# VectorE's blocks of a gated attention pair move into the score ring, local logits move one tile ahead, and the gate moves into the denominators

## The chip, the cores and the metric

The kernel runs on one core of one Trainium2 chip. The time is the device time of one execution in microseconds (us). Engines are written as in the profile: PE is TensorE (PEld its weight loads), ACT is ScalarE, DVE is VectorE, POOL is GpSimd, SP is the engine that issues the DMAs. Each engine works through a queue of its own in order, and they meet by semaphores.

## The reference

Two attention layers over the same 2048 rows of 512 numbers, with 32 heads of 16 each, are mixed by a gate per row. A is full attention, B looks at eight earlier rows, two apart. B's input is not `B_x` but the same `x`.

```python
x = A_x                                             # [1, 2048, 512], bf16
g = sigmoid((x * gate_w).sum(-1, keepdims=True))
# A: q, k, v = x @ A_wqkv, 32 heads of 16
a = softmax(q @ k.T * 16 ** -0.5) @ v               # per head, 2048 x 2048
a = a.reshape(B, S, D) @ A_wo
# B: q, k, v = x @ B_wqkv; row s sees rows s, s - 2, ..., s - 14 (those >= 0)
b = softmax(where(mask, q . k[s - 2 * w], -1e9) * ...) over w, times v[s - 2 * w]
b = b.reshape(B, S, D) @ B_wo
return g * a + (1 - g) * b
```

## The kernel before

**Layer A.** The rows are cut into 4 chunks of 512 queries, the heads into 8 groups of 4. A *period* is one chunk and one group, so there are 32 periods, chunk by chunk. In a period there are 64 *blocks*: one head's scores of 128 keys (16 key tiles) against 512 queries. A block's scores are one matmul with 32 rows of weights (`kt_all`) and fill one PSUM bank; four such matmuls on different rows of the array can run at once. Keys lie in partitions and queries along the free axis, so the exponentials need no transposition before they are multiplied with the values. A value tile has 16 columns and a column of ones, so that row 17 of the accumulator `acc` collects the denominators.

**The ring.** Scores for ScalarE go in turn into a set of three banks (`rA`) and a set of two (`rB`) (line 19, `qk` and `ex` at lines 962 to 971). ScalarE takes a set in one instruction (`pT<-ring`). The eight banks of PSUM are 3 + 2 for the ring, one for `acc`, and two under the name `misc`, through which everything else goes: projections of Q, K, V, of layer B, of the output, transposes, and the scores of VectorE's blocks.

**VectorE's blocks.** From period 4 on, 4, 8 or 12 of the 64 blocks (`n_dve`, 264 of 2048 in all, of the last three key tiles) get their exponential on VectorE (`d_group`, line 983). Each block's scores are a matmul into a `misc` bank (`dq`). `p1` turns them into a 16-bit logarithm in `dt` (128x512, one instruction a block). Four blocks make a group. Four shifts of it (`sh`, 128x2048, `pd<-dt`), each rounded to a bf16 pattern, are weighted by four copies of the values (`vd_all`) and added up in `acc`: 16 matmuls a group.

**End of a period.** VectorE transposes `acc` (`po1`), takes the reciprocal of the denominators and multiplies (`po2`), and transposes back once in two periods (`po3`). The output projection of layer A (`a_part`) is evicted with a factor `g` per row (`a_ev`, tile `fa`), that of layer B (`b_part`) is added (`b_ev`), and the sum is stored.

**Layer B** (`b_tile`, line 721) has 16 tiles of 128 rows. K and V are projected, evicted to `kvs` and stored in DRAM (`kv_scr`); the shifted rows are loaded from there (`ksh`, `vsh`, each in two halves of four shifts). GpSimd multiplies and adds up the logits (`logits_half`, tile `lg`, 128x256), VectorE takes maximum and difference (`sm_pre`, which starts with `mx`), ScalarE the exponential (`sm_exp`, in `lg`), VectorE sum, reciprocal and product (`sm_post`), GpSimd multiplies the values (`av_half`). The factor 1 - g is in `sm_post`. TensorE transposes the result for the output projection (`fin`, eviction `oe`).

**The gate.** One row of `x @ gate_w` per chunk is written to DRAM by way of VectorE (`zrow`), read back as 16 rows of 128, transposed, and goes through ScalarE's exponential (`zsig`) and three small VectorE instructions (`zgate`).

**The order.** Nothing is issued where it stands in the code. Each step becomes an `Op` with an engine, an estimated duration, a due time, and the buffers that it takes and frees. `list_schedule` (line 137) plays the estimates through: each time it takes the engine that can start first and on it the op with the earliest due time among those that can start soon. The result is a fixed order for each engine's queue; estimates have no other effect on the run. Where the planner sees TensorE idle or only little used, it adds matmuls on zeros (`idle`, `put`, `zeros`). Due times of layer A come from `UNIT` (us a block) and `T0`; those of layer B's tile t from `B0 + t * BSP`:

```python
CFG = dict(
    set_sizes=(3, 2),
    ...
    b_start=32.0,
    b_space=46.7,
```

All instructions of an engine are recorded in one helper line (292 for most, 301 for matmuls), so the profile is read by tile names.

Of the kernel before, what the change touches and what calls it, by code (L numbers as in the profile page):

```python
# [18 lines left out]
    set_sizes=(3, 2),  # L19
    n_dve=(0,) * 4 + (4, 8) * 2 + (8, 12) * 12,  # L20
    dve_tiles=3,
    b_start=32.0,
    b_space=46.7,
# [18 lines left out]
NPT = 3  # L42
# [39 lines left out]
WAVE = lambda n: PASS * n  # L82
AHEAD = dict(pe=0.10, dve=0.12, act=0.25, pool=0.5, sp=0.0)
# [53 lines left out]
def list_schedule(ops, zeros):  # L137
# [40 lines left out]
    out, extra = [], []  # L178
    while len(out) < len(ops):
# [37 lines left out]
        if e == "pe":  # L217
            o.t, end = arr.put(o, t)
            o.done = end + LAT[e] + o.lat
        else:  # L220
            occ = o.occ(t) if callable(o.occ) else o.occ
            o.t, o.done = t, t + max(occ, o.lat)
            free[e] = t + occ
        cand[e].remove(o)
        out.append(o)
        for s_ in succ.get(o, ()):
            left[s_] -= 1
            if left[s_] == 0:
                s_.ready = max([s_.rel] + [d.done for d in s_.deps] + [d.t for d in s_.after])
                cand[s_.eng].append(s_)  # L230
# [4 lines left out]
def kernel(  # L235
# [23 lines left out]
    SZ = cfg["set_sizes"]  # L259
# [6 lines left out]
    def misc_ps(shape, dtype=FP32, tag="misc"):  # L266
        return ps.tile(shape, dtype, tag=tag, bufs=2 if tag == "misc" else 1, name="misc_ps")
# [50 lines left out]
    def op(eng, occ, fn, dl, **kw):  # L318
        o = Op(eng, occ, fn, dl, **kw)
        ops.append(o)  # L320
        return o
# [8 lines left out]
    B0, BSP = cfg["b_start"], cfg["b_space"]  # L330
    UNIT = 0.445
# [4 lines left out]
    dorder = [(t, j) for t in range(NT - 1, NT - 1 - NTD, -1) for j in range(4)]  # L336
    n_dve = cfg["n_dve"]
    units, first_unit = [], []
    for pi, (c_, i) in enumerate(periods):
        dset = set(dorder[:n_dve[pi]])  # L340
        first_unit.append(len(units))
        units += [(pi, t, j) for t in range(NT) for j in range(4) if (t, j) not in dset]
    first_unit.append(len(units))
    sets = []
    u = 0
    while u < len(units):
        n = SZ[len(sets) % 2]
        sets.append(units[u:u + n])
        u += n
    S0 = [T0 + UNIT * f for f in first_unit]  # L350

    def in_b(t):
        return B0 <= t < B0 + 16.5 * BSP

# [9 lines left out]
    z_scr = tc.dram_tile([S], FP32, name="z_scr")  # L364
# [3 lines left out]
    identf = const.tile([NT, NT], FP32, name="identf")  # L368
# [12 lines left out]
    negk = const.tile([128, NG], FP32, name="negk")  # L381
    ott2 = const.tile([128, 2, BPC, 32], BF16, name="ott2")
    g_sp = const.tile([128, NT], FP32, name="g_sp")
    omg = const.tile([128, NT], FP32, name="omg")
# [54 lines left out]
    def load_w(part):  # L439
        def s():  # L440
            if part == 0:
                wst["q"] = work.tile([128, NGR, QW], BF16, name="wst", tag="pd", bufs=NPD)
                out = wst["q"][:]
            else:
                out = wkv[:, :, (part - 1) * D:part * D]
            SP.dma_start(out=out, in_=a_w3[:, :, part * D:(part + 1) * D])
        return s
# [6 lines left out]
    def load_wo():  # L454
        SP.dma_start(out=bwo[:], in_=B_wo.rearrange("(c p) n -> p c n", p=128))
        wo4 = A_wo.rearrange("(a e j d) n -> j e d a n", e=2, j=4, d=DH)
        for j in range(4):
            for e in range(2):
                SP.dma_start(out=woarr[32 * j + DH * e:32 * j + DH * (e + 1), :, :], in_=wo4[j, e])
        SP.dma_start(out=kv_scr[0:16, :], in_=zst["z"][0:16, :])  # L460
# [12 lines left out]
    o_wo = op("sp", 5.5, load_wo, -8.2, deps=[o_wz], use=[zt], lat=24.0)  # L473
# [25 lines left out]
    o_warm = op("pe", 4.0, warm, -9.0, deps=[o_init_d], alloc=[tok("misc", 2)])  # L499
# [34 lines left out]
    def k_proj(i, sc, tag, dl, rel=0.0):  # L534
        st = {}
        tk = tok(tag, 2 if tag == "misc" else 1)
# [16 lines left out]
    def k_bound(i, dl):  # L553
        st = {}
        tk = tok("misc", 2)
# [5 lines left out]
        def sw():  # L561
            st["p"] = misc_ps([128, 2])
# [21 lines left out]
    for i in range(NG):  # L584
        o_kc[i] = []
        for sc in range(NC):
            if i == 0:
                o_kc[i].append(k_proj(i, sc, ("misc", "acc", "misc", "misc")[sc], -2.0 + sc))
            else:
                o_kc[i].append(k_proj(i, sc, "misc", S0[i] - 8.0 - 4.5 * (NC - 1 - sc), rel=S0[i - 1] - 6.0 if i > 1 else 10.0))  # L590
        k_bound(i, 2.0 if i == 0 else S0[i] - 5.0)


    o_v = {}

    def v_proj(h0, h1, tb, TB, tag, dl, rel=0.0):
        n = (h1 - h0) * DH
        st = {}
        tk = tok(tag, 2 if tag == "misc" else 1)
# [12 lines left out]
        def ev():  # L612
            V.tensor_copy(out=vp_all[:, tb:tb + TB, h0:h1, 0:DH], in_=st["pv"][:].rearrange("p t (h d) -> p t h d", d=DH))
            for t in range(max(tb, NT - NTD), tb + TB):
                for m in range(NV):
                    V.tensor_scalar(out=vd_all[:, m, t - (NT - NTD), h0:h1, :], in0=vp_all[:, t, h0:h1, :],
                                    scalar1=WEIGHTS[m] * 2.0 ** -DEXP, scalar2=None, op0=ALU.mult)
        xs = [o for sc in range(NC) if sc * TPC < tb + TB and (sc + 1) * TPC > tb for o in o_xt[sc]]
        a = op("pe", 0.62, mk(0), dl - 2.0, full=2, deps=[o_wv] + xs, alloc=[tk], rel=rel, name=f"vp{h0}.{tb}")
        b = op("pe", 0.62, mk(1), dl - 1.4, full=2, deps=[a], use=[tk])  # L620
        c = op("dve", 0.61 + 0.9 * max(0, min(TB, tb + TB - (NT - NTD))), ev, dl, deps=[b, o_init_p], use=[tk])
        for h in range(h0, h1):
            for t in range(tb, tb + TB):
                o_v[(h, t)] = c

    v_proj(0, 4, 0, 8, "misc", 3.0)
    v_proj(0, 4, 8, 8, "misc", 4.0)
# [9 lines left out]
    def q_proj(pi, tag, dl, rel=0.0):  # L637
        c_, i = periods[pi]
        st = {}
        tk = tok(tag, 2 if tag == "misc" else 1)  # L640
# [29 lines left out]
    o_zd = []  # L670
    for sc in range(NC):
        st = {}
        tk, tz = tok("misc", 2), tok("accT", 2)

        def zc(sc=sc, st=st):
            st["p"] = misc_ps([1, QW])
            for c in range(DC):
                mm(st["p"][0:1, :], gw[:, c:c + 1], xT[:, c, sc * QW:(sc + 1) * QW], c == 0, c == DC - 1, tile_position=(0, 0))

        def ze(st=st):  # L680
            zr = work.tile([128, BPC, 32], FP32, name="zrow", tag="accT", bufs=2)
            st["z"] = zr[0:1].rearrange("p b d -> p (b d)")
            V.tensor_copy(out=st["z"], in_=st["p"][0:1, :])

        def zd(sc=sc, st=st):
            SP.dma_start(out=z_scr[sc * QW:(sc + 1) * QW].rearrange("(o n) -> o n", o=1), in_=st["z"])
        dl = 32.0 + 2 * sc
        a = op("pe", 0.9, zc, dl, full=4, deps=[o_bw] + o_xt[sc], alloc=[tk], rel=22.0)
        b = op("dve", 0.61, ze, dl + 1, deps=[a], alloc=[tz], use=[tk])
        o_zd.append(op("sp", 0.6, zd, dl + 2, deps=[b], use=[tz]))  # L690
    st_g = {}
    tzr, tzp = tok("zrows", 1), tok("misc", 2)

    def zfin():
        st_g["zrows"] = work.tile([NT, 128], FP32, name="zrows", tag="zrows", bufs=1)
        SP.dma_start(out=st_g["zrows"][:], in_=z_scr.rearrange("(t p) -> t p", p=128))

    def ztr():
        st_g["zp"] = misc_ps([128, NT])
        chain(nc.tensor.transpose(out=st_g["zp"][:, 0:NT], in_=st_g["zrows"][:], identity=identf[0:NT, 0:NT]))  # L700
# [8 lines left out]
    a = op("sp", 0.6, zfin, 41.0, deps=o_zd, alloc=[tzr], lat=3.0)  # L709
    a = op("pe", 0.15, ztr, 42.0, deps=[a, o_init_p], alloc=[tzp], use=[tzr])  # L710
    a = op("act", 0.25, zsig, 43.0, deps=[a], use=[tzp])
    o_g = op("dve", 0.8, zgate, 44.0, deps=[a])
# [8 lines left out]
    def b_tile(t):  # L721
        st = {}
        tb = B0 + t * BSP
# [24 lines left out]
        tk = tok("misc", 2)  # L748
        a = op("pe", WAVE(2), proj("pk", 1, 0), tb - 34, full=2, deps=[o_bw] + o_xt[cb], alloc=[tk, tkv], rel=rel)
        a = op("pe", WAVE(2), proj("pk", 1, 2), tb - 33.5, full=2, deps=[a], use=[tk])  # L750
        ka = op("dve", 0.61, ke, tb - 33, deps=[a], use=[tk, tkv])
        tk = tok("misc", 2)
        a = op("pe", WAVE(2), proj("pv", 2, 0), tb - 32, full=2, deps=[o_bw] + o_xt[cb], alloc=[tk], rel=rel)
        a = op("pe", WAVE(2), proj("pv", 2, 2), tb - 31.5, full=2, deps=[a], use=[tk])
        va = op("dve", 0.61, ve, tb - 31, deps=[a, ka], use=[tk, tkv])
        o_kvd.append(op("sp", 0.6, kvd, tb - 30, deps=[va], use=[tkv], lat=3.0))
# [5 lines left out]
        tk = tok("misc", 2)  # L762
        a = op("pe", WAVE(2), proj("pq", 0, 0), tb - 24, full=2, deps=[o_bw] + o_xt[cb], alloc=[tk, tqb], rel=rel)
        a = op("pe", WAVE(2), proj("pq", 0, 2), tb - 23.5, full=2, deps=[a], use=[tk])
        qa = op("dve", 0.61, qe, tb - 23, deps=[a], use=[tk, tqb])
# [10 lines left out]
        kvd_ = o_kvd[max(0, t - 1):t + 1] + [o_wo]  # L776
        lk = [op("sp", 0.7, load("ksh", 0, hf), tb + (-24, 4)[hf], deps=kvd_, alloc=[tks[hf]], lat=7.0) for hf in range(2)]
        lv = [op("sp", 0.7, load("vsh", 1, hf), tb + (18, 30)[hf], deps=kvd_, alloc=[tvs[hf]], lat=7.0) for hf in range(2)]

        def logits_half(hf):  # L780
            def s():
                if hf == 0:
                    st["lg"] = work.tile([128, H, W], FP32, name="lg", tag="lg", bufs=2)
                ksh, lg, qb = st["ksh", hf], st["lg"], st["qb"]
                prod = work.tile([128, WP, D], FP32, name="prod", tag="prod", bufs=1)
                pv_ = prod[:].rearrange("p w (h d) -> p w h d", d=DH)
                for wp in range(0, WH, WP):
                    for w_ in range(WP):
                        for c0 in range(0, D, HB):
# [418 lines left out]
```

## Time and profile before

| | |
|---|---|
| Time, median of 3 runs | 916.61 us (915.06 to 917.93) |
| The profiled execution | 922.33 us, span of the core 920.6 us |
| Granted clock of TensorE, mean | 0.942 |
| ScalarE busy | 824.5 us (90%), of it 815.5 in 714 exps of the ring |
| TensorE busy (modelled) | 787.3 us (86%) |
| GpSimd busy | 777.8 us (84%) |
| VectorE busy | 686.9 us (75%) |
| DMA | 47.34 MB, 51 GB/s over the span |

A group's row has its busy time, the mean duration of one instruction, and the idle time of its engine just before such instructions with what ended most of it. Instructions of one engine overlap at their ends, so a group's busy time is a little less than the count times the mean. TensorE's busy time is modelled. A row of the waits names who waited, for whom, how long in total, how often, and the longest. The granted clock is TensorE's share of full speed.

### The profile page before, as it was taken

What the parts mean: (1) busy time and instruction counts of PE and PEld (TensorE: products, weight loads), DVE (VectorE), ACT (ScalarE), POOL (GpSimd) and SP (SyncE); (2) the same over time, 40 slices, a digit from 0 to 9 for tenths busy, and PEclk for the clock granted to TensorE, in tenths of its full rate; (3) what the DMA queues carried; (4) which work ended last, traced back from release to release, by engine and by line L of the source; (5) the groups of instructions that cost most, each with busy time, mean ns of one, the idle gap of its engine ahead of it and who ended that gap; (6) DMA issues with size and microseconds to landing.
All of it is one profiled execution on the core that took longest, in us unless ns stands there. A gap on an engine that the chain in (4) does not pass through costs nothing. (4 is left out here: it accounts for less than half of the span.)

```text
span 920.6 us, 18113 instructions
## 1 busy us (share of the span) xinstructions
PE 787.3 (86%) x7025; PEld 249.3 (27%) x7025; DVE 686.9 (75%) x1107; ACT 824.5 (90%) x736; POOL 777.8 (84%) x1088
## 2 busy tenths in 40 slices
PE   8988989898888898887878888798888988888787
PEld 4333323233222222222222222222222222213122
DVE  4456484856867978898878878778877978888766
ACT  2999999996989999999988979889988979889796
POOL 4559998997989788799998979999799989999840
PEclk9999999998989999999998999989997989979799
DMA  8310202021020002102020110201210111200000
GB/s 272 109 59 24 82 24 81 23 69 36 24 81 12 30 23 88 58 23 81 25 80 29 31 63 29 80 24 37 68 59 23 59 58 35 81 20 28 1 1 24
DMA packets 44477, 47.34 MB, mean 51 GB/s; under 512 B 2372, under 2 KB 41812, under 8 KB 44392
## 3 DMA queue, kind: packets, MB, share of 16 engines
q1 hardware_dynamic: 44392, 46.19, 15.6%
q8 instruction: 55, 0.90, 0.4%
q14 instruction: 30, 0.25, 0.1%
HBM read 39.86 MB, written 6.33 MB: 50 GB/s over the span
## 5 line engine op out<-in xcount | busy, mean ns | idle before, releaser
L292 ACT ACTIVATE pT<-ring 128x1536 bf16<-128x1536 f32 x714 | 815.5, 1320 | 52.8 <-PE ring L301 33.7
L301 PE MATMUL ring<-qt,kt_all 32*128 32x512 bf16 x1784 | 295.6, 397 | 80.2 <-ACT pT L292 75.1
L292 POOL TENSOR_TENSOR prod<-prod 128x256 f32<-128x256 f32 x352 | 269.2, 772 | 10.0
L292 DVE TENSOR_SCALAR pd<-dt 128x2048 uint16<-128x2048 uint16 x264 | 258.1, 1020 | 5.2 <-PE acc L301 3.6
L301 PE MATMUL acc<-pT,vp_all 128*17 128x512 bf16 (+1 forms) x1784 | 233.4, 401 | 1.3 <-DVE accT L292 1.2
L292 POOL TENSOR_TENSOR prod<-vsh,lg 128x256 f32<-128x256 bf16 x256 | 185.7, 755 | 45.7 <-issue 35.2
L292 POOL TENSOR_TENSOR prod<-ksh,qb 128x256 f32<-128x256 bf16 x256 | 188.7, 767 | 33.2 <-DMA ksh<-kv_scr 20.7
L292 DVE TENSOR_SCALAR dt<-misc 128x512 uint16<-128x512 f32 x264 | 172.6, 684 | 52.1 <-PE misc L301 37.6
L301 PEld LDWEIGHTS <-kt_all 32*128 32x128 bf16 x2048 | 98.8, 91 | 368.8 <-issue 358.9
L301 PE MATMUL acc<-pd,vd_all 128*17 128x512 bf16 x1056 | 105.5, 394 | 13.0 <-DVE pd L292 12.8
L301 PE MATMUL misc<-qt,kt_all 32*128 32x512 bf16 x264 | 92.3, 402 | 10.6 <-DVE dt L292 6.5
L301 PE MATMUL acc<-z 128*32 128x512 bf16 x276 | 99.4, 423 | 0.0
L301 PEld LDWEIGHTS <-vp_all 128*17 128x17 bf16 (+1 forms) x1784 | 53.8, 89 | 70.0 <-issue 55.9
L301 PE MATMUL misc_ps<-bw,xT 128*128 128x512 bf16 x192 | 61.1, 412 | 8.2 <-DVE dt L292 7.9
L292 POOL TENSOR_TENSOR ob<-ob,prod 128x256 f32<-128x256 f32 x64 | 54.0, 845 | 5.0
L301 PEld LDWEIGHTS <-vd_all 128*17 128x17 bf16 x1056 | 27.8, 88 | 64.2 <-issue 60.3
L301 PE MATMUL misc_ps<-xT,wq 128*32 128x512 bf16 x512 | 41.3, 389 | 0.0
L301 PE MATMUL misc_ps<-xT,wkv 128*32 128x512 bf16 x384 | 39.6, 385 | 1.9 <-DVE vp_all L292 1.0
L301 PEld LDWEIGHTS <-z 128*32 128x32 bf16 x312 | 26.1, 99 | 53.9 <-issue 45.6
L301 PEld LDWEIGHTS <-xT 128*128 128x128 bf16 x512 | 28.8, 100 | 41.7 <-issue 38.0
L301 PE MATMUL misc_ps<-xT,wk 128*32 128x512 bf16 x128 | 36.9, 386 | 0.0
L292 DVE CAST kvs<-misc_ps 128x512 bf16<-128x512 f32 x32 | 22.0, 688 | 19.8 <-PE misc_ps L301 19.5
(78 smaller groups left out, 510.0 us busy)
## 6 DMA issues: line engine op xcount, KB each, us to landing
ksh<-kv_scr SPq DMA_DIRECT2D x32, 512.0 KB, 4.4
vsh<-kv_scr SPq DMA_DIRECT2D x32, 512.0 KB, 4.0
kv_scr<-kvs SPq DMA_DIRECT2D x16, 256.0 KB, 2.6
xld<-in_A_x_dram SPq DMA_DIRECT2D x4, 512.0 KB, 8.7
out_dram<-osb SPq DMA_DIRECT2D x16, 128.0 KB, 1.7
bw<-in_B_wqkv_dram SPq DMA_DIRECT2D x1, 1536.0 KB
wkv<-in_A_wqkv_dram SPq DMA_DIRECT2D x2, 512.0 KB, 9.0
wst<-in_A_wqkv_dram SPq DMA_DIRECT2D x1, 512.0 KB, 8.5
```

What stands on the lines that cost most here:

```text
L292: return chain_on(key, f(*a, **k))
L301: return chain(nc.tensor.matmul(out, lhsT=lhsT, rhs=rhs, start=start, stop=stop, **kw))
```

## The change

- **Ring.** Both ring sets have three banks; `misc` has one bank. In each of 264 sets the third bank holds one block of VectorE's, at most one a set, spread over the period (`SPREAD`). ScalarE takes the first two banks of such a set, VectorE's `p1` the third (`d_set`, which replaces `d_group`). `SPREAD` and the last three key tiles set which block goes where. The block's scores are one of the set's three matmuls; there is no matmul into `misc` for it.
- **Buffers.** `pT` has 5 buffers in one pool in place of 3 + 3. From period 8 on, the space of the projection weights `wkv`, which are used up by then, holds two more `dt`, so that there are three.
- **Layer B.** The logits of both halves are due before the tile's date, a whole tile ahead of the values (`L1`, `KL`), and the planner allows for margins around the softmax (`SM_LAT`). GpSimd's steps are planned in pieces; its instructions are the same. Loads wait for the zero rows of `kv_scr` alone and no longer for the output weights, whose load moves behind.
- **Gate.** It is computed in columns by 64 small matmuls, without DRAM. 16 more spread it to the layout of the denominators (`g_rw`); `po2` multiplies the reciprocals by it. The output projections of A and B then add up in one accumulation (`ab_part`) with one eviction.
- **Planner.** Other estimates (`BESIDE`, `UNDER`: VectorE's shifts and GpSimd slow each other), due times and spacing (`UNIT`, `b_space`). The built program has 683 exps of the ring (418 of three banks, 265 of two) for 714, and 671 matmuls on zeros for 312.

```diff
-    set_sizes=(3, 2),
+    set_size=3,
...
-    b_start=32.0,
-    b_space=46.7,
+    b_start=40.0,
+    b_space=(41.0,) * 4 + (44.5,) * 4 + (47.5,) * 8,
...
-NPT = 3
+NPT = 5
+LATE0 = 8
+NDL = 3
+SPREAD = (0.85, 0.95)
...
+L1, KL, SM_LAT = -13.0, (-24.0, -20.0), (1.0, 1.0, 0.3, 1.0)
+SH_LAT = 0.3
+BESIDE, UNDER = 0.575, 0.52
...
+P1D, SHD = -100.0, 1.0
...
-        return ps.tile(shape, dtype, tag=tag, bufs=2 if tag == "misc" else 1, name="misc_ps")
+        return ps.tile(shape, dtype, tag=tag, bufs=1, name="misc_ps")
...
-    UNIT = 0.445
+    UNIT = 0.465
...
+            if len(cur) == SZ - 1 and due < n and due < n * taken / (SPREAD[n // 12] * total):
...
+                    cur.append((pi, *dl_[due][1], gi))
...
+    dt_bufs = [dt_a[:]] + [b_.bitcast(U16) for b_ in spare[:NDL - 1]]
...
+    def zmm(sc):
+        def s():
+            if sc == 0:
+                st_g["zp"] = misc_ps([128, NT])
+            for t in range(sc * TPC, (sc + 1) * TPC):
+                for c in range(DC):
+                    mm(st_g["zp"][:, t:t + 1], xT[:, c, t * 128:(t + 1) * 128], gw[:, c:c + 1], c == 0, c == DC - 1)
...
-        kvd_ = o_kvd[max(0, t - 1):t + 1] + [o_wo]
-        lk = [op("sp", 0.7, load("ksh", 0, hf), tb + (-24, 4)[hf], deps=kvd_, alloc=[tks[hf]], lat=7.0) for hf in range(2)]
+        kvd_ = o_kvd[max(0, t - 1):t + 1] + [o_zr]
+        lk = [op("sp", 0.7, load("ksh", 0, hf), tb + KL[hf], deps=kvd_, alloc=[tks[hf]], lat=7.0) for hf in range(2)]
...
-        l0 = op("pool", 11.6, logits_half(0), tb - 14, deps=[lk[0], qa], alloc=[tlg], use=[tks[0], tqb], name=f"lg{t}")
-        l1 = op("pool", 11.6, logits_half(1), tb + 18, deps=[l0, lk[1]], use=[tks[1], tqb, tlg])
-        a = op("dve", 0.95, sm_pre, tb + 19, deps=[l1], use=[tlg])
-        a = op("act", 0.36, sm_exp, tb + 18, deps=[a], use=[tlg])
-        a = op("dve", 1.95, sm_post, tb + 21, deps=[a, o_g], use=[tlg])
-        a0 = op("pool", 10.1, av_half(0), tb + 40, deps=[a, lv[0]], alloc=[tob], use=[tlg, tvs[0]])
+        l0 = chain_ops(lgs[0], tb - 14, [lk[0], qa], [tlg], [tks[0], tqb])
+        l1 = chain_ops(lgs[1], tb + L1, [l0, lk[1]], [], [tks[1], tqb, tlg])
+        a = op("dve", 0.95, sm_pre, tb + SMD, deps=[l1], use=[tlg], lat=0.95 + SM_LAT[1])
+        l1.lat += SM_LAT[0]
+        a = op("act", 0.36, sm_exp, tb + SMD, deps=[a], use=[tlg], lat=0.36 + SM_LAT[2])
+        a = op("dve", 1.95, sm_post, tb + SMD, deps=[a, o_g], use=[tlg])
+        a0 = chain_ops(avs[0], tb + 40, [a, lv[0]], [tob], [tlg, tvs[0]])
...
+    def d_set(pi, gi, t, j, st, q_, tr_, tn):
...
+        def p1():
+            V.tensor_scalar(out=g["dt"][:, n_, :], in0=st["r"][:, q_, :], scalar1=float(DH) ** -0.5 * RES / LN2,
+                            scalar2=(127.0 + DEXP + SHIFT * float(DH) ** -0.5 / LN2) * RES, op0=ALU.mult, op1=ALU.add)
...
+        o = op("dve", 0.61, p1, tn + P1D, deps=deps, alloc=[g["td"]] if first else [], use=[tr_] + ([] if first else [g["td"]]),
+               after=[d_last[0]], name=f"p1_{pi}")
...
+        def dur(t):
+            return 0.605
...
-        tp = tok("pT" + ring, NPT)
+        tp = tok("pT", NPT)
...
+            V.tensor_tensor(out=rden[:], in0=rden[:], in1=g_rw[:, c_ * BPC:(c_ + 1) * BPC], op=ALU.mult)
...
-            V.tensor_scalar(out=st["fa"], in0=st["pf"][:], scalar1=g_sp[:, t:t + 1], scalar2=None, op0=ALU.mult)
...
+                for k in range(k0, min(k0 + 2, DC + nh)):
+                    if k < DC:
+                        mm_ct(st["pf"], obt_tiles[c_][:, k, tt * 128:(tt + 1) * 128], bwo[:, k, :], k == 0, k == DC + nh - 1)
+                    else:
+                        mm_ct(st["pf"], oat_tiles[c_][:, k - DC, tt * 128:(tt + 1) * 128], woarr[:, k - DC, :], False,
+                              k == DC + nh - 1)
```

## The prediction

> **What bounds it now.** I read the page's busy shares first, then its costliest groups, then the waits, then the busy time in chosen stretches. ScalarE, which does 1784 of the 2048 blocks of exponentials, is the fullest engine:
>
> ```profile
> PE 787.3 (86%) x7025; PEld 249.3 (27%) x7025; DVE 686.9 (75%) x1107; ACT 824.5 (90%) x736; POOL 777.8 (84%) x1088
> ...
> L292 ACT ACTIVATE pT<-ring 128x1536 bf16<-128x1536 f32 x714 | 815.5, 1320 | 52.8 <-PE ring L301 33.7
> L292 DVE TENSOR_SCALAR pd<-dt 128x2048 uint16<-128x2048 uint16 x264 | 258.1, 1020 | 5.2 <-PE acc L301 3.6
> L292 POOL TENSOR_TENSOR prod<-vsh,lg 128x256 f32<-128x256 bf16 x256 | 185.7, 755 | 45.7 <-issue 35.2
> L292 DVE TENSOR_SCALAR dt<-misc 128x512 uint16<-128x512 f32 x264 | 172.6, 684 | 52.1 <-PE misc L301 37.6
> ```
>
> Each group shows its busy time, the mean of one, and the idle time before it. ScalarE's first exp starts at 24.2 us and its last ends at 912.1, so what can be gained lies in its idle time between: 52.8 - 7.5 (the first wait) before the exps, and 23.3 before the local softmax's exps, 68.6 in all. By form the 3-bank exps are 547.2 us for 357 (1.533 each) and the 2-bank ones 394.6 for 356 (1.109). The waits name the second idle term:
>
> ```profile
> DVE mx L292 <- POOL lg L292: 32.0, 10, 5.4
> ACT lg L292 <- DVE lg L292: 23.3, 10, 4.1
> ```
>
> Ten times VectorE stands still until GpSimd has finished a tile's local logits. It is one queue, so TensorE, which waits for its evictions, and ScalarE stop too. Busy time in nine stretches around nine of these waits, against ten stretches far from any (one row of each, then each sum; columns PE, PEld, DVE, ACT, POOL, granted clock, DMA share, GB/s):
>
> ```profile
> 590.00:606.00 16.00, 10.65 (x73) 2.25 (x64) 10.06 (x17) 9.28 (x10) 15.06 (x25) 0.68 0.12 33
> ...
> sum 127.00, PE 94.39 PEld 22.31 DVE 89.66 ACT 83.62 POOL 101.58; mean PE 10.49 PEld 2.48 DVE 9.96 ACT 9.29 POOL 11.29
> ...
> 616.00:682.00 66.00, 58.03 (x512) 17.80 (x512) 54.79 (x79) 65.91 (x60) 59.06 (x79) 1.00 0.12 38
> ...
> sum 430.00, PE 380.04 PEld 126.61 DVE 330.89 ACT 426.99 POOL 390.03; mean PE 38.00 PEld 12.66 DVE 33.09 ACT 42.70 POOL 39.00
> ```
>
> At granted clock 1.00 ScalarE is 99% busy (426.99 of 430), with VectorE up to 90% busy beside it (52.58 of 58 in 370 to 428). In the nine stretches it is busy 83.62 of 127, and the clock is 0.57 to 0.89. So 43 us of the 68.6 hang on one coupling: wait, TensorE idle, half clock, late scores.
>
> **The change part by part.**
>
> *Exps.* The built order has 418 three-bank and 265 two-bank exps for 357 and 356 (and one of a single bank). The busy row gives 815.5/714 = 1.142 for a mean of 2.5 banks; the forms differ by 0.424 a bank; so 1.354 and 0.930. 418 x 1.354 + 265 x 0.930 = 812.4: **-3 us**, on the path.
>
> *Local logits a tile ahead.* GpSimd's order becomes logits(t+1), then values(t), so the softmax of t has a whole tile of GpSimd work before anyone needs it, and the change puts margins ahead of its VectorE steps. Is GpSimd early enough? A tile costs it, by its rows, (188.7 + 192 x 0.832 + 29.7 + 24.8)/16 = 25.2 us of logits and (185.7 + 96 x 0.832 + 54.0 + 27.1 + 24.8)/16 = 23.2 of values. Ahead of the last softmax stand 16 logits and 14 values: from its start at 33.1 that ends at 761. ScalarE's order has that softmax behind 1613 of 1784 blocks: 24.2 + 1613 x 0.457 = 761 without any loss, later with every loss of its own. So level at worst, early in practice: the nine stretches return to the rate of the others. **-43 us** (bounds 0, if GpSimd is still last, and -43). By rows alone the exchange is between 23.3 (the waits themselves) and 43 (with the slow clock behind them). [...] GpSimd's own 47 us of waits for the softmax ("issue" 35.2 in its row, and others) go too, off the path.
>
> *VectorE's blocks in the ring.* Before, each of the 264 blocks had a score matmul of its own into `misc`, 92.3 us of modelled matmul time that stood between ring refills. Now it is one of three matmuls of a set on different rows of the array, so it costs TensorE about nothing. Of the other idle time of ScalarE, 68.6 - 43.4 = 25, part comes from these matmuls and their bank (TensorE waited 6.5 us for `dt` before them and 8.1 before projections). Between 0 and 25 goes; I take half, **-13**.
>
> The price: a bank set is refilled only when VectorE too has read it. From scores to need, ScalarE covers its own exp and the next, 0.93 + 1.35 (or 0.93 + 0.93 where two such sets follow); VectorE's read takes 172.6/264 = 0.65 and the refill 0.40, so 0.8 to 1.2 us may be lost in its queue. I went along VectorE's new order from block to block, its work by its rows (0.65 a block, 0.98 a shift, 0.66 an eviction) against the exps' time between those sets: what exceeds the allowance adds up to 53 us for an allowance of 0.3, 23 for 0.9, 16 for 1.2. Bounds 0 and 53, **+20**. Only 67 of the 264 refills wait for VectorE by name; elsewhere an earlier wait for a later shift covers it. Behind a waiting refill stand the values' matmuls and the projections in TensorE's queue, and ScalarE waits for all of it. VectorE's total hardly moves: -12 `fa` evictions (8.9 us), -4 `zrow` (2.7), +32 products on 16 columns (0.2 each), all under its idle time of 230 us.
>
> *One bank for projections.* In the first four periods (114 us of exps) some 50 groups of matmuls share it, each about 1.28 on TensorE (41.3/32, 61.1/48) and 0.69 to evict: about 100 us in a row. It fits if nothing slips: **+4**, bounds 0 and +15. Queued behind a late eviction are the next scores in TensorE's queue, so ScalarE pays. [...] No run here has yet shown one bank.
>
> *Fillers.* A wave of matmuls costs 0.22 us of issue (the trace has 0.39 for one wave and 0.61 for two). Matmuls on zeros go from 312 to 671, 359 x 0.22 = 79 us, where the planner sees TensorE idle; the 264 score matmuls and 31 sets that go are 295 x 0.22 = 65 us. Nearly even, so no term: their cover is TensorE's idle time, and where that is gone each costs its 0.22.
>
> *Start.* VectorE has one more `vp_all` and one more `qt` eviction ahead of the first scores (0.69 each): **+1.5**, bounds 0 and +3.
>
> *At nothing:* the gate by small matmuls in place of five DMAs (between 30 and 50 us, under exps); weight loads of the output projections behind the zero rows on SP, still before the first tile's stores; the larger identity on GpSimd, before its first logits at 33.1; the fused output projection and tail (the last evictions 0.69 for 0.74, four times).
>
> Sum: -3 -43 -13 +20 +4 +1.5 = -33.5. The profiled execution took 922.33 us (span 920.6), the median is 916.61, 0.6% less. 922.3 - 33.5 = 888.8, times 0.9938: **883 us**.
>
> **The rivals.**
>
> *Everything comes off.* Gating and bank cost nothing, all 25 of the other idle time goes: 922.3 - 3 - 43 - 25 + 1.5 = 852.8, **848**. For it: 99% busy at full clock with VectorE at 90%. Against: 49 blocks come late even with 0.9 allowed.
>
> *GpSimd is still last* (the change doesn't do what it says). Late tiles cost it 27 + 24 us (logits 763.7 to 777.7 and 736.4 to 750.6, values 712.2 to 736.3). At that pace the last logits end at 33 + 16 x 27 + 14 x 24 = 801; before, 63.8 us followed theirs (856.8 to 920.6) with 111 blocks left, now 171: 801 + 63.8 + 60 x 0.457 = 892, **888**, and up to **900** if the clock drops at the waits. Against: early tiles took 45.
>
> *The single bank and the clock eat it.* The waits go (-23), but late evictions of the one bank leave TensorE idle in their place and the slow clock stays: 922.3 - 3 - 23 - 13 + 20 + 15 + 1.5 = 919.8, **914**, no change or a little faster. For it: the 100 us of bank time in 114; against: the three undisturbed stretches before 265 us ran at clock 1.00 with VectorE only 57 to 75% busy (44.33 of 78 to 31.47 of 42). [...]
>
> *VectorE becomes what releases the ring* (slower). If most blocks find one shift ahead of them: 1.02 + 0.68 + 0.40 = 2.10 against 1.86 between two such sets, 0.24 x 264 = 63 in place of 20, with nothing of the 13: 922.3 - 3 - 43 + 63 + 4 + 1.5 = 944.8, **939**. It decides from about 0.15 us a block on (264 x 0.15 = 40, which is 3 + 43 - 4 - 1.5). For it: shifts are 39% of VectorE's time after 260 us. Against: the order puts each block first as soon as its scores are planned.
>
> **How the numbers follow.** Chances: forecast 0.48 (own range 862 to 900), all comes off 0.15, GpSimd last 0.13, bank and clock 0.08, VectorE 0.16. A difference under 0.3% (2.7 us) is about what can't be told from none: the fourth case is split 0.05 faster, 0.03 same. Faster 0.81, same 0.03, slower 0.16. The range 846 to 918 leaves out a third of the second case and nearly all of the last.
>
> **What would show it.** Right: no wait of `mx` for GpSimd's `lg` beyond 5 us in all; ScalarE's exps about 812 us busy with 30 to 40 idle; mean granted clock over 0.95; VectorE over 78% busy. Gating shows as ring matmuls waiting for the blocks' reads on VectorE (about 20 us), the bank as projections waiting for evictions before 150 us. Wrong: `mx` still waiting for `lg`, or the ring waiting for VectorE by more than 50 us.

## The result, and the profile after

The changed kernel takes 955.74 us (median of 4 runs, 952.01 to 961.8) against 917.13 us for the kernel before (915.06 to 917.93, 4 runs): ratio 1.043, 95% interval 1.037 to 1.049. It is slower where 883 us was predicted. The profiled execution took 952.01 us, with a span of 950.1 us and a mean granted clock of 0.985 (0.942 before).

From the page of the changed kernel, busy shares and then groups (busy time, mean of one, idle time before):

```profile
PE 799.8 (84%) x7463; PEld 273.0 (29%) x7463; DVE 670.4 (71%) x1120; ACT 834.2 (88%) x705; POOL 771.1 (81%) x1088
...
L315 ACT ACTIVATE pT<-ring 128x1536 bf16<-128x1536 f32 (+1 forms) x683 | 826.3, 1305 | 94.1 <-DVE wkv L315 31.4
...
L315 DVE TENSOR_SCALAR wkv<-ring 128x512 uint16<-128x512 f32 x160 | 110.0, 688 | 119.9 <-PE ring L324 80.6
...
L315 DVE TENSOR_SCALAR dt_a<-ring 128x512 uint16<-128x512 f32 x104 | 70.9, 684 | 41.7 <-ACT pT L315 21.2
```

VectorE's reads of its blocks are in two rows here, because their results lie in `wkv` (160) and `dt_a` (104). The shifts have not become slower (144.8 + 95.8 us in their two rows, against 258.1), and VectorE is less busy than before. ScalarE's exps stand idle for 94.1 us in place of 52.8. By form the idle time sits before the two-bank exps, that is the sets that ScalarE shares with VectorE:

```profile
L315 ACT ACTIVATE pT<-ring 128x1536 bf16<-128x1536 f32 x418 | 586.2, 1483 | 19.2 <-PE ring L324 13.9 <-PE acc L324 5.0
L315 ACT ACTIVATE pT<-ring 128x1024 bf16<-128x1024 f32 x265 | 266.9, 1025 | 75.0 <-DVE wkv L315 31.4 <-DVE dt_a L315 25.6 <-PE acc L324 9.8
```

The waits (who waited for whom, total, times, longest):

```profile
DVE wkv L315 <- ACT pT L315: 38.5, 35, 1.7
...
ACT pT L315 <- DVE wkv L315: 31.4, 56, 1.4
...
ACT pT L315 <- DVE dt_a L315: 25.6, 36, 2.9
PE ring L324 <- DVE wkv L315: 21.6, 34, 1.2
DVE dt_a L315 <- ACT pT L315: 21.2, 20, 1.8
...
PE ring L324 <- DVE dt_a L315: 15.1, 25, 1.2
```

The old waits are gone: no `mx` waits for `lg`, no `lg` for VectorE. In their place exps wait for VectorE's reads (57.0 us), and reads wait for exps (59.7 us). Neither was foreseen, for an exp reads banks 0 and 1 of a set and VectorE's read bank 2. The timeline shows one of each (start, duration, what; idle time before it and what ended it):

```profile
520.83 0.69 DVE L315 TENSOR_SCALAR wkv<-ring 128x512 uint16<-128x512 f32 x1
...
521.62 4.62 ACT L315 ACTIVATE pT<-ring 128x1024 bf16<-128x1024 f32 x4 [0.31 <-DVE wkv L315]
...
524.93 0.69 DVE L315 TENSOR_SCALAR wkv<-ring 128x512 uint16<-128x512 f32 x1 [0.93 <-ACT pT L315]
...
525.68 0.39 PE L324 MATMUL ring<-qt,kt_all 32*128 32x512 bf16 x3 [0.93 <-DVE wkv L315]
```

At 521.52 a read ends, and only 0.1 us later the exp of the same set starts, after 0.31 us of standstill. Then the other way round: VectorE stands still for 0.93 us until an exp has ended, reads for 0.69, and only then is the set refilled, with TensorE idle for 0.93 before it.

The built program says the same in full. Of the 264 shared sets, 196 have a semaphore wait at the exp for the read of its own set, and 68 have one at the read for the exp of its own set. The framework that turns the kernel into queues and semaphores has put an order between the two reads of each of these sets, although they go to different banks; the first in the written order goes first (with the exp written first throughout, in run 4, no exp waits for VectorE). In the trace the read starts first in 196 pairs and the exp in 68, not one of the 264 pairs overlaps, and from the start of the first to the end of the second a pair takes 1.81 us (median). The planner knows nothing of it.

The profile of before already held the sign, at its start, where ScalarE copies one bank of a tile `pxt` and VectorE the next:

```profile
7.33 1.01 ACT L292 COPY xT<-pxt 128x1024 bf16<-128x1024 bf16 x1 [5.31 <-PE pxt L512]
8.37 0.69 DVE L292 COPY xT<-pxt 128x1024 bf16<-128x1024 bf16 x1 [0.84 <-ACT xT L292]
...
10.35 1.01 ACT L292 COPY xT<-pxt 128x1024 bf16<-128x1024 bf16 x1 [2.01 <-PE pxt L512]
...
11.39 0.69 DVE L292 COPY xT<-pxt 128x1024 bf16<-128x1024 bf16 x1 [2.33 <-ACT xT L292]
```

VectorE's copies start 0.03 us after ScalarE's end, and the row names ScalarE as what ended the wait.

As a ledger from first to last exp: 887.9 us before (24.2 to 912.1), 916.8 after (24.6 to 941.4), +28.9. That is -23.3 of idle time before the softmax's exps, +42.6 before the ring's exps (45.3 to 87.9, the wait before the very first left out), +10.8 of busy time of theirs (an exp that starts after a standstill does not overlap the end of the one before; the sum of the durations less the busy row, that is the overlap, is 127.1 us before and 65.2 after), and -1.2 of ScalarE's other work. The two profiled executions are 29.7 us apart (922.33 and 952.01), the medians 38.6, so about 9 us of the difference stand in no row here.

### The profile page after: what moved, and what is told of

Same layout as the page of the kernel before. It is cut to its first block, busy times and chain, and to the rows that moved or that the text cites. A ratio compares the mean times of both kernels' runs of the same rounds, so it can differ in the third digit from the quotient of the medians.

```text
span 950.1 us, 18895 instructions
## 1 busy us (share of the span) xinstructions
PE 799.8 (84%) x7463; PEld 273.0 (29%) x7463; DVE 670.4 (71%) x1120; ACT 834.2 (88%) x705; POOL 771.1 (81%) x1088
## 4 chain that ended last, share of the span: by engine, by line
ACT 35%; DVE 32%; PE 16%; issue 15%; DMA 1%; ACTq 0%; SPq 0%; DVEq 0%
ACT pT L315 34%; DVE pd_a L315 9%; DVE wkv L315 7%; PE misc_ps L324 7%; PE ring L324 6%; DVE dt_a L315 5%; PE acc L324 4%; DVE qt L315 1%; DVE vd_all L315 1%; DVE lg L315 1%; DVE accT L315 1%; DVE rden L315 1%; DVE ott L315 1%; DVE kvs L315 1%; DMA xld<-in_A_x_dram 1%
## 5 line engine op out<-in xcount | busy, mean ns | idle before, releaser
L315 ACT ACTIVATE pT<-ring 128x1536 bf16<-128x1536 f32 (+1 forms) x683 | 826.3, 1305 | 94.1 <-DVE wkv L315 31.4
L324 PE MATMUL ring<-qt,kt_all 32*128 32x512 bf16 x2048 | 270.0, 385 | 113.7 <-ACT pT L315 69.8
L315 POOL TENSOR_TENSOR prod<-prod 128x256 f32<-128x256 f32 x352 | 268.9, 771 | 10.1
L324 PE MATMUL acc<-pT,vp_all 128*17 128x512 bf16 (+1 forms) x1784 | 192.0, 390 | 3.6 <-DVE accT L315 3.2
L315 DVE TENSOR_SCALAR wkv<-ring 128x512 uint16<-128x512 f32 x160 | 110.0, 688 | 119.9 <-PE ring L324 80.6
L324 PE MATMUL misc_ps<-z 128*32 128x512 bf16 x578 | 178.9, 389 | 1.9 <-DVE z L315 1.6
L315 DVE TENSOR_SCALAR pd_a<-wkv 128x2048 uint16<-128x2048 uint16 x160 | 144.8, 930 | 2.1 <-PE acc L324 1.1
L324 PE MATMUL acc<-pd_a,vd_all 128*17 128x512 bf16 x1056 | 109.7, 383 | 5.2 <-DVE pd_a L315 4.1
L315 DVE TENSOR_SCALAR dt_a<-ring 128x512 uint16<-128x512 f32 x104 | 70.9, 684 | 41.7 <-ACT pT L315 21.2
L315 DVE TENSOR_SCALAR pd_a<-dt_a 128x2048 uint16<-128x2048 uint16 x104 | 95.8, 951 | 0.7
L324 PEld LDWEIGHTS <-z 128*32 128x32 bf16 x671 | 58.9, 96 | 68.2 <-issue 33.5
L324 PEld LDWEIGHTS <-vd_all 128*17 128x17 bf16 x1056 | 30.9, 88 | 48.4 <-issue 40.8
## 6 DMA issues: line engine op xcount, KB each, us to landing
bw<-in_B_wqkv_dram SPq DMA_DIRECT2D x1, 1536.0 KB, 12.6
```

The source lines that it names most:

```text
L315: return chain_on(key, f(*a, **k))
L324: return chain(nc.tensor.matmul(out, lhsT=lhsT, rhs=rhs, start=start, stop=stop, **kw))
```

## The experiments

Theory 1: the two reads in a row are what costs. Rivals: VectorE's queue is late and holds the ring anyway; the single projection bank; the added matmuls on zeros. The later runs ask what the other parts of the change are worth. Each ratio is against the kernel before, run on the same chip (medians 921.05, 919.05 and 918.94 us for runs 1 to 4, 5 to 8 and 9 to 12). The clock is the mean granted clock of the profiled execution.

| run | us, median of 4 | ratio, 95% interval | clock |
|---|---|---|---|
| the changed kernel | 955.74 | 1.043 (1.037 to 1.049) | 0.985 |
| 1 reads apart | 894.93 | 0.973 (0.969 to 0.976) | 0.979 |
| 2 before, logits ahead | 910.45 | 0.989 (0.985 to 0.993) | 0.947 |
| 3 changed, no fillers | 975.89 | 1.060 (1.055 to 1.064) | 0.912 |
| 4 changed, exp first | 965.94 | 1.050 (1.044 to 1.055) | 0.983 |
| 5 reads apart, logits not ahead | 912.12 | 0.991 (0.989 to 0.993) | 0.968 |
| 6 before, logits ahead, GpSimd's durations | 895.94 | 0.974 (0.971 to 0.977) | 0.958 |
| 7 changed, row in the plan | 956.51 | 1.039 (1.034 to 1.043) | 0.976 |
| 8 reads apart, 280 blocks | 902.43 | 0.981 (0.979 to 0.984) | 0.983 |
| 9 before, GpSimd's durations | 901.30 | 0.979 (0.976 to 0.983) | 0.964 |
| 10 before, gate folded | 938.98 | 1.021 (1.018 to 1.023) | 0.936 |
| 11 run 6 with the gate folded | 890.63 | 0.968 (0.965 to 0.971) | 0.975 |
| 12 reads apart, 248 blocks | 895.61 | 0.974 (0.971 to 0.977) | 0.982 |

### 1. The reads apart

`i1` is VectorE's read of a set, `i2` its exp. The order between the two is taken out, and the next refill waits for both by name.

```diff
+    def apart(st):
+        if "i1" in st and "i2" in st:
+            for x, y in (("i1", "i2"), ("i2", "i1")):
+                tc.declare_no_dep(st[x].ins, st[y].ins, reason="they read different banks")
...
+                if s_ == 0 and "i1" in held.get(ring, ()):
+                    for x in ("i1", "i2"):
+                        tc.add_manual_dep(m_.ins, held[ring][x].ins.name, sync_dep, reason="bank set read")
+            held[ring] = st
```

> The changed kernel (955.7 us) with one thing undone: in the 264 bank sets that ScalarE and VectorE share, the exp (banks 0 and 1) and VectorE's read (bank 2) no longer wait for each other; the next refill of the set waits for both by name. Order of every engine, work and sizes are the same. Theory 1, the two reads in a row are what costs: the two-bank exps' idle time of 75 us falls below 30, no exp waits for VectorE by name, and the time falls by 60 to 100 us, to 855-895. Rival, VectorE's queue is late and holds the ring anyway: the same wait comes back as ring matmuls waiting for VectorE (now 21.6 + 15.1 us, then 80 or more), time 940-956. Rival, the single bank for projections or the added matmuls on zeros hold TensorE: time 945-956, exps idle behind TensorE's ring matmuls.

Measured: 894.93 us, 61 us less than the changed kernel, at the upper edge of theory 1's 855 to 895, and faster than the kernel before by 2.4 to 3.1%. Its two-bank exps by form, then its waits:

```profile
L315 ACT ACTIVATE pT<-ring 128x1024 bf16<-128x1024 f32 x265 | 276.7, 1078 | 22.3 <-PE acc L324 12.6 <-PE ring L324 9.3
```

```profile
PE ring L324 <- DVE wkv L315: 3.6, 5, 1.0
...
PE ring L324 <- DVE dt_a L315: 3.1, 4, 1.2
...
PEld L324 <- DVE dt_a L315: 2.5, 3, 1.5
...
PEld L324 <- DVE wkv L315: 0.5, 1, 0.5
```

The idle time before two-bank exps falls from 75.0 to 22.3 us, and no exp waits for VectorE. The wait does not come back at the ring: all waits of a refill for VectorE come to 9.7 us (weight loads included, which now carry some of the waits). 233 of the 264 pairs overlap, for 90.7 us in all, and a pair takes 1.44 us in place of 1.81. Theory 1 stands. The rival of the late queue does not, nor do bank and fillers as causes of the loss, since all of that is the same in this kernel. One stretch of each kernel (columns PE, PEld, DVE, ACT, POOL, granted clock, DMA share, GB/s), the changed one and then this one:

```profile
450.00:550.00 100.00, 82.90 (x718) 26.75 (x716) 77.03 (x111) 85.76 (x76) 95.92 (x133) 0.98 0.14 48
```

```profile
450.00:550.00 100.00, 92.17 (x819) 28.26 (x824) 84.46 (x129) 96.47 (x86) 96.08 (x126) 1.00 0.15 49
```

ScalarE goes from 85.76 to 96.47 us busy of 100, with VectorE busier beside it.

### 4. Exp first

```diff
-        deps = [st["qk"]]
+        deps = [st["qk"], st["ex"]]
```

> The changed kernel with VectorE's read of a shared set always behind the set's exp (in 196 of 264 sets it had been ahead of it, and the exp waited). Reads stay in a row. If ScalarE's direct waits for VectorE (31.4 + 25.6 us before the two-bank exps) are what costs and the longer hold of the set does not: 890-915. If the row itself costs, because exp, read and refill then follow one another (0.93 + 0.68 + 0.40 us against 0.93 to 1.35 of the next exp): 940-980, with ring matmuls waiting for VectorE over 100 us in place of exps that wait for it.

Measured: 965.94 us. No exp waits for VectorE any more, and yet the kernel is no faster than the changed one. The waits:

```profile
DVE wkv L315 <- ACT pT L315: 105.6, 78, 4.4
ACT pT L315 <- PE ring L324: 86.8, 117, 6.3
DVE dt_a L315 <- ACT pT L315: 52.8, 45, 4.4
...
PE ring L324 <- DVE dt_a L315: 22.3, 40, 2.6
PE ring L324 <- DVE wkv L315: 18.9, 47, 1.7
```

VectorE waits for exps (158.4 us), so the set is read out later and exps wait for scores (86.8). That refills would wait for VectorE by name for over 100 us was a miss: it is 41.2, and most of the delay shows at the engines on either side. The row itself costs, whichever comes first.

### 7. The row in the plan

Exp and read of one set take turns at a token of their own, so that the planner counts both in a row.

```diff
-        st["ex"] = op("act", 0.05 + 0.4267 * n, ex, tn, deps=[a], alloc=[tp], use=[tr_], name=f"ex{k}")
+        st["ex"] = op("act", 0.05 + 0.4267 * n, ex, tn, deps=[a], alloc=[tp, tok(f"rd{k}", 1)], use=[tr_], name=f"ex{k}")
```

The read gets the same token.

> The changed kernel (955.7 us), reads of a shared set still in a row, but the planner knows it: exp and VectorE's read of one set may not overlap in its plan. If the row costs mostly because the plan did not know of it: 910-935. If it costs by itself (264 times exp, read and refill in a row): 940-965, exps still idle for 70 us and more before the two-bank forms.

Measured: 956.51 us, the changed kernel's time within the intervals. The exps' waits for VectorE fall to 40.1 us (21.1 + 19.0), and those for scores rise from 15.5 to 49.8. The idle time before two-bank exps is 54.5 us, not the 70 and more that was expected; before three-bank ones it rises from 19.2 to 43.0. An order that knows of the row does not buy it back here.

### 3. No fillers

```diff
-        return t0, min(4, int(room / PASS), int(-(-lack // 1)))
+        return t0, 0
```

> The changed kernel without the planner's matmuls on zeros in the projection bank (502 of 671 matmuls on zeros go; those inside the accumulator's groups stay). If these hold TensorE or the one projection bank: 20-60 us faster, 895-935. If the two reads in a row are the cause: between 945 and 965, the clock a little lower (0.93-0.98), exps waiting for VectorE's blocks by name as before.

Measured: 975.89 us, slower than the changed kernel, with a clock of 0.912. Matmuls on zeros fall from 671 to 282, not to 169 as expected: those in the accumulator's groups rise from 93 to 279. Exps still wait for VectorE (34.6 + 28.5 us). The fillers do not hold TensorE; without most of them 15 to 20 us more are lost (by the ratios and by the medians). The clock is lower than the 0.93 that theory 1 allowed, and the time 11 us above its range.

### 2, 9 and 6. Logits ahead and GpSimd's durations, on the kernel before

Run 2 moves the logits, run 9 changes the durations in the plan alone, run 6 has both.

```diff
-        lk = [op("sp", 0.7, load("ksh", 0, hf), tb + (-24, 4)[hf], deps=kvd_, alloc=[tks[hf]], lat=7.0) for hf in range(2)]
+        lk = [op("sp", 0.7, load("ksh", 0, hf), tb + (-24, -20)[hf], deps=kvd_, alloc=[tks[hf]], lat=7.0) for hf in range(2)]
...
-        l1 = op("pool", 11.6, logits_half(1), tb + 18, deps=[l0, lk[1]], use=[tks[1], tqb, tlg])
-        a = op("dve", 0.95, sm_pre, tb + 19, deps=[l1], use=[tlg])
+        l1 = op("pool", 11.6, logits_half(1), tb - 13, deps=[l0, lk[1]], use=[tks[1], tqb, tlg])
+        a = op("dve", 0.95, sm_pre, tb, deps=[l1], use=[tlg], lat=0.95 + 1.0)
```

In runs 9 and 6 GpSimd's four steps are planned at 12.6, 12.6, 11.0 and 12.2 us (48.4 a tile, as their rows add up to) for 11.6, 11.6, 10.1 and 11.2 (44.5).

> The kernel before (916.6 us) with only the local logits moved a tile ahead (second half of the logits and its loads before the values of the tile before, softmax due later); rings, banks, VectorE's blocks and gate as before. The prediction priced this part at -43 us, bounds 0 and -43. If that holds: 872-880, waits of mx for lg under 5 us, clock over 0.97. If the ten waits were only where a lateness showed that has another cause: 905-917 with other waits in their place. If GpSimd is the last in any case: 900 or more, with mx still waiting for lg.

> The kernel before with only GpSimd's durations in the plan raised (12.6 + 12.6, 11.0 + 12.2 us); the local logits stay where they were. Order alone gave -10, order and durations together -23. If the two add: 903-909. If the durations do it by themselves: 893-900. If only both together take the waits away, because without the order the values of a tile still wait for a softmax that nothing covers: 912-922, mx still waiting 20 us or more for lg or GpSimd for the softmax.

> The kernel before with the local logits a tile ahead, as in the second run (910.5 us, where mx still waited 27 us for lg), and with GpSimd's durations in the plan raised to those of its rows (12.6 + 12.6 us for the logits, 11.0 + 12.2 for the values, in place of 11.6 + 11.6, 10.1 + 11.2). If the second run fell short because the plan asked for the softmax earlier than GpSimd can give it: mx waits under 10 us, clock over 0.96, 880-900. If the order of the logits is worth no more than its -10: 905-917, with TensorE's single reasons for idling in place of the wait.

Measured, as differences to the kernel before: order alone -10.6 us (within the second case's time, but with the third case's sign, `mx` still waiting for `lg`), durations alone -17.6 (between two of its cases), both -23.1 (within the first, with the clock at 0.958 where over 0.96 was expected). The wait that the prediction was about, in runs 2, 9 and 6:

```profile
DVE mx L292 <- POOL lg L292: 27.0, 10, 6.7
```

```profile
DVE mx L292 <- POOL lg L292: 8.0, 7, 2.3
```

```profile
DVE mx L292 <- POOL lg L292: 6.3, 6, 2.3
```

The order alone leaves most of the wait: the plan still asks for the softmax at a pace that GpSimd does not keep. The larger part of the gain lies in estimates that agree with the trace; on top of them the order adds 5 us (the intervals of runs 6 and 9 overlap a little, so this is not settled). In run 6 the idle time before the softmax's exps is 0.1 us, 23.2 less than before, and that before the ring's exps 51.3, against 52.8. What comes off is the waits themselves; most of the slow-clock part, which the term of 43 us had counted with them, does not (mean clock 0.958, against 0.942 before).

### 5. Reads apart, logits not ahead

```diff
-L1, KL, SM_LAT = -13.0, (-24.0, -20.0), (1.0, 1.0, 0.3, 1.0)
+L1, KL, SM_LAT = 18.0, (-24.0, 4.0), (0.0, 0.0, 0.0, 0.0)
```

The softmax is due at 18 to 21 us after the tile's date again.

> The kernel of the run with the reads apart (894.9 us) with the local logits put back: second half of the logits and its loads behind the values of the tile before, softmax due as before and without margins; GpSimd's durations in the plan stay the changed kernel's. The prediction priced the move at -43 us (bounds 0 and -43), so undoing it should give 925-940, with ten or so waits of mx for lg, 20-35 us, and a clock of 0.93-0.96. The run of the kernel before with only this part gave -10: by that 900-908. If the plan's longer durations for GpSimd are what removed the waits, and not the order: 893-900, with mx waiting less than 8 us.

Measured: 912.12 us, between the cases: 17 us more than run 1, with 10.0 us of waits of `mx` and 9.7 of ScalarE for `lg`. Beside the reads apart the move is worth about 17 us.

### 10 and 11. The gate folded

The gate's code, `po2` and `ab_part` of the change are put into the kernel before (run 10) and into run 6's kernel (run 11), with two projection banks as before.

```diff
+            V.tensor_tensor(out=rden[:], in0=rden[:], in1=g_rw[:, c_ * BPC:(c_ + 1) * BPC], op=ALU.mult)
```

> The kernel before with only the gate folded into the denominators (gate by small matmuls in place of five transfers, one fused output projection a tile; two projection banks as before). The prediction took it at nothing: 914-920, a difference under 0.3%. If the shorter eviction chain of the output (12 evictions and 12 bank turns fewer, 8.9 us of VectorE) is worth something: 908-913. If the waits move to the earlier gate: 920-926.

> The kernel before with the local logits a tile ahead and GpSimd's durations raised (895.9 us in the sixth run), and the gate folded: all of the change but the blocks in the ring and the single bank. If these two bring nothing once the reads are apart, this equals the run with the reads apart: 891-898. If the blocks in the ring were worth the 13 us that the prediction gave them, this stays 10 us or more behind that run: 903 or more.

Run 10 takes 938.98 us, 20 more than before, which no case had. Its waits:

```profile
POOL prod L292 <- issue: 60.1, 16, 8.8
...
DVE mx L292 <- POOL lg L292: 38.1, 12, 5.8
...
ACT lg L292 <- DVE lg L292: 31.8, 10, 5.0
```

Before, these were 38.2, 32.0 and 23.3 us. The plan now puts the softmaxes on average 11 blocks earlier in ScalarE's order, about 5 us, and GpSimd's logits end later than before from the fourth tile on. That this shift of the plan explains all 20 us is argued, not shown. With the logits ahead and the durations right, the gate costs nothing: run 11 takes 890.63 us (ratio 0.968 against 0.974; the intervals touch, so a gain of its own is not settled). It is the fastest kernel here, and it has neither VectorE's blocks in the ring nor the single bank. The mark for blocks that are worth 13 us was 903 or more; no run shows a gain from them, even with the reads apart (0.973 in run 1 against 0.968 here, and the intervals overlap).

### 8 and 12. More and fewer blocks

```diff
-    n_dve=(0,) * 4 + (4, 8) * 2 + (8, 12) * 12,
+    n_dve=(0,) * 4 + (4, 8) * 2 + (8, 12, 12) * 8,
```

Run 12 has `(8, 8, 12) * 8`.

> The kernel with the reads apart (894.9 us) with 280 of 2048 blocks on VectorE instead of 264. ScalarE has 16 blocks fewer, 16 x 0.457 = 7 us; VectorE 16 reads and 16 shifts more, 16 x (0.68 + 0.95) = 26 us on 677. If ScalarE's work is the bound: 886-891. If VectorE's queue holds the ring now that it is free of the row: 895-905.

> The kernel with the reads apart (894.9 us) with 248 blocks on VectorE instead of 264 (280 gave 902.4, with GpSimd in 56% of the chain that ended last). ScalarE has 16 blocks more, +7 us; VectorE 26 us less, and GpSimd less shared time. If ScalarE sets the end: 898-904. If VectorE's and GpSimd's load is what holds it: 885-892.

Measured: 902.43 us with 280 blocks, 894.93 with 264, 895.61 with 248. Refills hardly wait for VectorE in run 8 either (4.6 + 3.8 us at the matmuls, 3.9 at the weight loads), so the ring is not what makes 280 slower; its exps wait 34.5 us for `acc`, against 18.8 in run 1. In both runs the chain that ended last is more than half GpSimd (56 and 63%; 13% in run 1). Neither engine's work alone sets the end: the cases had been drawn too simply.

## Why the prediction was wrong

**The step that failed** is the price of *VectorE's blocks in the ring* (+20, bounds 0 and 53). It took for granted that exp and VectorE's read of a set run side by side from the moment the scores land, and priced only a late queue of VectorE. Read one after the other, they cost 61 us (the changed kernel against run 1; 65 by the two ratios). The sentence "Only 67 of the 264 refills wait for VectorE by name; elsewhere an earlier wait for a later shift covers it" read the built order wrongly: most of the other refills need no wait for VectorE because the exp before them has already waited for it. ScalarE's own waits, in the same built order, would have shown 196 of them. The price as meant, a set held by a late VectorE, is 9.7 us of waits in run 1, below the 20.

**The rival that VectorE releases the ring** (939 us, chance 0.16) has the right side and comes within 17 us of the time, but not by its mechanism, so that nearness is luck. Refills wait 36.7 us for VectorE at the matmuls, below the mark of 50; the rest shows as exps that wait for VectorE and reads that wait for exps. VectorE is 71% busy and not over 78.

**Local logits a tile ahead**, -43: the wait of `mx` is gone and the clock is over 0.95, as forecast, but the order does not do it by itself, and the size was not right. In run 2 the order alone leaves 27.0 of the 32.0 us of `mx`; in run 9 the durations alone leave 8.0. The order alone is worth -10 to -17, together with GpSimd's durations -23. The prediction had the waits themselves at 23.3 and counted the half clock behind them as well, as if it had no other cause. No run shows the 43 us; run 6 gives the smaller figure: the waits go (23.2 us of idle time before the softmax's exps), and the mean clock rises from 0.942 to only 0.958. That the clock falls because TensorE has stood idle was the author's estimate from the nine stretches. The profile of before bears it out only in part: at 133.8 us the granted clock is 0.51 (mean to 137.0) with no idle time of TensorE over 1.5 us ahead of it, so the half clock also comes without a long wait; what leads there is open.

**The gain of 13** from blocks that need no matmul of their own: not shown. The idle time before the ring's exps in run 1 is 47.5 us, against 52.8 before, but it is 43.9 in run 11, which has no blocks in the ring. **Exps**, -3: the busy row is 815.2 us in run 1 against 815.5, so nothing (in the changed kernel +10.8, see the ledger); durations by form change with how closely exps follow each other (below).

**One bank**, +4: not isolated. GpSimd's first product starts at 37.7 us, after VectorE's `qb`, in place of 33.1; no run separates the rest. **Fillers** at nothing: they cost nothing, and without most of them 15 to 20 us more are lost. **Start**, +1.5: the first exp starts 0.4 us later (1.9 in run 1). **The gate** at nothing: so in run 11, but +20 alone on the kernel before, where the order around GpSimd was fragile.

In the rival of GpSimd as the last, the two ranges that it names add up to 28.2 us of logits a tile, not 27, which would put it some 19 us later.

Without the row the sum comes near: -33.5 us forecast, -26.1 measured in run 1, and its 894.93 us lies in the forecast's own range of 862 to 900. That is in part luck, for the terms missed on both sides: the logits brought 10 to 23 us and not 43, the 13 is not shown, and in place of 20 there are 9.7 us of waits.

## What to carry to other kernels

When two engines are to share a buffer, read the waits of both in the built program, not only those of the engine that refills it: an order between two reads appears nowhere in the kernel's code, and a planner that does not know of it cannot plan for it. Look for a small place in the old profile where the same pairing already runs, such as two copies out of one PSUM tile. Before moving work to hide a wait, compare the planner's durations with the rows of the trace: here correct estimates alone gave 17.6 us, more than the move.

## What the runs showed of the hardware

In run 1 ScalarE and VectorE read different banks of PSUM at the same time without slowing each other. VectorE's read takes 0.684 us on average in run 1, where 233 of 264 overlap the exp of their set, and 0.686 in the changed kernel, where none does. Exps that each start before the one ahead has ended start 0.904 us apart with two banks and 1.331 with three (medians of run 1), whether VectorE reads PSUM beside them for over 0.6 us, for less, or not at all; in the kernel before the medians of these three cases are 0.903, 0.903 and 0.904 with two banks, and 1.330 each with three. The order that the built program of the changed kernel keeps between the two reads of a set is stricter than run 1 needed.

In these profiles the row of an exp is longer when exps follow each other closely: a three-bank exp has 1.533 us before, 1.523 in run 1 and 1.483 in the changed kernel, where ScalarE waits more; a two-bank one 1.109, 1.078 and 1.025. Within run 1 a three-bank exp that starts before the end of the one ahead takes 1.529, and one that starts later 1.451; in the kernel before 1.544 and 1.450. So the mean duration of an exp here counts part of the neighbour's time: before, a three-bank exp is 1.533 us long, and the next, where it follows closely, starts 1.330 us after its start.
